# Attention inside a transformer block: each product with V preceded by one transpose of the next head's probabilities, and the small memory products moved to the steps without products with V

## The chip, the cores and the metric

The kernel runs on one core of a Trainium2 chip. The metric is the device time of one execution in microseconds (us). Times of the kernel before are the median of three runs; profiles are of one execution each. Engines are called as in the profile: PE is TensorE (its matmuls), PEld its loads of weights (the operand that stays in the array), DVE is VectorE, ACT ScalarE, POOL GpSimd, SP the engine that issues most transfers.

## What is computed

Layer norm, attention with a compressive memory, the output projection with its residual, and then a feed-forward block. The change is in the attention: 32 heads of 32 columns, four segments of 512 tokens, and within a segment a softmax over the segment's own keys, plus a reading of a memory that the earlier segments have filled.

```
def _A_ref(x, wq, wk, wv, wo, beta):
    B, S, D = x.shape
    H = 32; Dh = D // H; N = 4; L = S // N
    ...
    for s in range(N):
        qs, ks, vs = q[:, :, s], k[:, :, s], v[:, :, s]
        logits = jnp.einsum("bhqd,bhkd->bhqk", qs, ks) * scale + mask
        p = _softmax(logits, axis=-1)
        a_dot = jnp.einsum("bhqk,bhkd->bhqd", p, vs)
        pq = phi(qs)
        num = jnp.einsum("bhld,bhde->bhle", pq, M)
        den = jnp.einsum("bhld,bhd->bhl", pq, z)[..., None] + 1e-6
        a_mem = num / den
        o = g * a_mem + (1.0 - g) * a_dot
        outs.append(o)
        pk = phi(ks)
        M = M + jnp.einsum("bhld,bhle->bhde", pk, vs)
        z = z + jnp.einsum("bhld->bhd", pk)
    ...
    return o @ wo
```

Each segment reads M and z as the segments before it left them; the first reads nothing that counts, and the last need not write.

## The kernel before

All matrix work is done in float32 accuracy by halves: an operand is split into an upper part (names ending in h) and the rest (ending in l), and a product is the sum of the products of the parts.

The sequence is done in two halves of 1024 tokens, each of two segments. A **unit** is four heads (a group g of eight) of one segment, so there are 32 units. While the projections of one unit run on PE (`dense`: 24 steps t = 0 to 23, eight each for keys, queries and values, each step three 128x512 matmuls, L124 to L126, into `kps`, `qps`, `vps`), the heads of the unit before it are worked on in between: `interleave` takes one step of `dense`, then one step of `heads`, in turn. A head has six steps of its own (`slot`), and a head's work is spread over three such slots, so that three heads are under way at a time, one slot apart.

What is done in which step is set by the table `HEAD`: `q1=3.2` means that operation q with argument 1 is done in step 3 of a head, at place 2 among that step's operations; a time of 6 to 12 is one slot later, 12 to 18 two slots later. The operations:

- `q` (0 to 3): one block of 128 rows of the logits, a matmul into `pqk` (L659), DVE's scaling, mask and row extreme into `pr` (L660), ACT's exponential in place (L668). Block i has 128(i+1) keys.
- `t` (0 to 2): the transposes of the probabilities. Ten 128x128 blocks lie on or under the diagonal; they are turned on PE one by one (`ppt`, L709, against the identity `ident`) in groups of 4, 4 and 2, each group into one PSUM bank (two banks in turn, tag `pt`). After a group ACT copies it to `pth` (L711), and later `s` lets DVE compute the rest `ptl` (L716).
- `a` (0, 1): the products with V, eight matmuls for a head into `po` (L729), of 512, 512, 384, 384 columns in `a0` and 128, 128, 256, 256 in `a1`. The operand in the array is a 128x64 piece of `vs`.
- `o`: the sum of the halves of `po` and, with the fourth head, the gate and the addition of the memory's part. `w` is a small transpose `pw` (L688) with the fourth head, `r` the reciprocals.

**Small memory products** (L425): a unit that reads the memory has 12 matmuls `pm` (128x132), a unit that writes it 12 matmuls `pmm` (128x128). They are not done where they arise: `dense` puts them on a list `small` (the read at time 25 of the table `TIMES`, counted in steps from the unit's start, the update at time 40), and `one_small()` takes the next one from the list, if there is one. It is called ahead of each transpose (ten times a head) and ahead of each product with V but one (seven times a head). Two places empty the list in one go: `query_halves` (time 20) takes all that are left, and `memory_turn` (time 35) what the read still lacks. PE carries its instructions out in the order in which this recording writes them.

Of the kernel before, what the change touches and what calls it, by code (L numbers as in the profile page):

```python
# [17 lines left out]
P = 128  # L18
# [12 lines left out]
VT, KT, OT = True, True, True  # L31
WLC = 8
TIMES = dict(pk=10, kx=12, pkh=21, pkl=22, ks=11, qs=16, pq=16, pqh=20, pql=20, omt=20, vx=24, pm=25, vs=32, vl=33, pmm=40, om=35, omc=40, od=62, lk=13, lq=16, lv=20, ck=18, cq=22, cv=28)
HEAD = dict(r=6.1, q0=1.1, a0=14.1, s2=14.2, t0=8.3, q2=2.4, s0=8.5, a1=15.1, q1=3.2, t1=10.1, w=9.2, q3=4.3, t2=11.1, o=17.2, s1=11.3)
KD, QD = 0, 3
SCALE = DH ** -0.5
EPS = 1e-5
# [6 lines left out]
def raw(ap):  # L44
    return ap.bitcast(F32)


def build(tc, x, wq, wk, wv, wo, beta, w1, b1, w2, b2, out):
# [304 lines left out]
    def attention(half, first):  # L353
# [59 lines left out]
        def one_small():  # L413
            if small:
                small.pop(0)()
# [280 lines left out]
        def ptr(st, n):  # L696
            grp = ((0,), (1, 3), (2,))[n]
            if n == 0:
                st["pth"] = ab.tile([P, 1280], F32R, name="pth", bufs=2)
                st["ptl"] = ab.tile([P, 1280], F32R, name="ptl", bufs=2)  # L700
            pr, pth, ptl = st["pr"], st["pth"], st["ptl"]
            ppt = psum.tile([P, 512], F32, tag="pt", name="ppt", bufs=2)
            base = koff[grp[0]]
            w = 0
            for jk in grp:
                for i in range(jk, 4):
                    one_small()
                    o = koff[jk] - base + (i - jk) * P
                    nc.tensor.transpose(ppt[:, o:o + P], pr[:, offs[i] + jk * P:offs[i] + (jk + 1) * P], ident)  # L709
                    w += P  # L710
            acts["pth"] = n, nc.scalar.copy(pth[:, base:base + w], ppt[:, :w])  # L711
            st["sub", n] = (ptl[:, base:base + w], ppt[:, :w], raw(pth[:, base:base + w]))

        def sub(st, n):
            o, x0, x1 = st["sub", n]
            nc.vector.tensor_tensor(o, x0, x1, op=ALU.subtract)  # L716

        def av(st, n):
            u, j = st["u"], st["j"]
            if n == 0:  # L720
                st["po"] = psum.tile([P, 512], F32, tag="av", name="po", bufs=1)[0:64, :]
            po = st["po"]
            for jk in (0, 1) if n == 0 else (3, 2):
                w = 512 - P * jk
                v = u["vs"][:, 4 * j + jk, :]
                for part in ("pth", "ptl"):
                    if (jk, part) != (3, "ptl"):
                        one_small()
                    nc.tensor.matmul(po[:, P * jk:], v, st[part][:, koff[jk]:koff[jk] + w],  # L729
                                     start=(jk, part) == (0, "pth"), stop=(jk, part) == (2, "ptl"))  # L730
            if n == 1:
                if j == 0:
                    u["ot"] = ab.tile([P, 512], F32, name="ot", bufs=1)
                nc.scalar.copy(u["ot"][32 * j:32 * j + 32, :], po[32:64, :])
# [24 lines left out]

        stages = int(max(HEAD.values())) // 6  # L760
        pipe = [None] * stages
        fns = {"q": qk, "r": inverse, "w": weigh, "t": ptr, "s": sub, "a": av, "o": av_out}

        def slot(cur):
            states = [cur] + pipe
            for step in range(6):
                for _, op in sorted((t % 6, op) for op, t in HEAD.items() if int(t) % 6 == step):
                    st = states[int(HEAD[op]) // 6]
                    if st:
                        fns[op[0]](st, *[int(c) for c in op[1:]])  # L770
                yield
            pipe[:] = states[:-1]

        def heads(u):
            for j in range(4):
                yield from slot({"u": u, "j": j})

        def tail():
            for _ in range(stages):
                yield from slot(None)  # L780
# [682 lines left out]
    for half in range(2):  # L1463
        acts["zt"] = zt = tc.alloc_tile_pool(name=f"zt{half}", bufs=1, side="right")
        attention_pool(half)
        first = None if half else opening()
        rest = attention(half, first)
        hts = [lnp.tile([P, D], F32, tag="ln", name="ht0", bufs=4) for _ in range(4)]
        ab = acts["ab"]
# [132 lines left out]
```

## Time and profile before

| what | value |
| --- | --- |
| median of three runs | 2272.93 us (2271.5 to 2276.78) |
| span of the profiled execution | 2272.7 us |
| attention, first half of the sequence | about 46 to 490 us of the span |
| attention, second half | about 945 to 1390 us |
| transposes `ppt` | 1280 |
| products with V `po`, L729 | 1024 |
| small products `pm` and `pmm` | 288 and 288 |

How the views are read: the groups give, for a line, engine, operation and shape, the count, then the busy time in us and the mean duration of one in ns, then the idle time of the engine before them. A PE matmul's own duration there counts from its start to the end of its flow through the array, and the matmuls overlap: a 128x512 one is listed with some 390 ns although the next one ends 0.23 us after it. What a matmul adds to the time is therefore read from the chain of waits, which lists, in order of time, when each piece of work began to be the last thing that held the end up, and for how long: start in us, length in us, engine, tile and line, and a count where neighbours are merged.

### The profile page before, as it was taken

Reading aid. Unit: us, or ns where it says so; the run is one execution under the profiler, and the core shown is the slowest. Engines: PE = TensorE matmul, PEld = TensorE weight load, DVE = VectorE, ACT = ScalarE, POOL = GpSimd, SP = SyncE. Lnnn points to the kernel's source line nnn. Section 1 sums busy time; section 2 is a strip of 40 time slices with the busy share of each in tenths; the row PEclk is TensorE's granted clock in tenths of the full one; section 3 lists DMA queues with packets and bytes.
Section 4 is the critical chain, followed back from the end, with each engine's and each line's share of the span. In section 5 each row is a group of like instructions: output and inputs, shape, how many; then the busy total and the mean of one; then the engine's idle time right before and its main releaser. Section 6 shows DMA issues by size and latency. Waiting matters only on the chain.

```text
span 2272.7 us, 34849 instructions
## 1 busy us (share of the span) xinstructions
PE 2243.7 (99%) x11481; PEld 1861.9 (82%) x11481; DVE 1541.0 (68%) x3073; ACT 1232.8 (54%) x2553; POOL 856.8 (38%) x710
## 2 busy tenths in 40 slices
PE   8999999999999999999999999999999999999999
PEld 6888888877888888888888887888888888888887
DVE  6777777776656565777777787655666766567653
ACT  6777777774453445777777775453334223222221
POOL 4232233334244442233333334244445654055430
PEclk9999999999999999999999999999999999999999
DMA  6666666665475655666655565466568975476762
GB/s 215 182 190 181 181 179 176 177 177 196 139 212 165 189 167 173 195 177 179 178 173 169 178 195 189 142 210 181 162 177 310 331 253 197 155 257 226 244 234 89
DMA packets 400798, 437.41 MB, mean 192 GB/s; under 512 B 33102, under 2 KB 267114, under 8 KB 400618
## 3 DMA queue, kind: packets, MB, share of 16 engines
q1 hardware_dynamic: 337450, 398.48, 56.8%
q10 hardware_dynamic: 63168, 36.71, 5.4%
q8 instruction: 91, 1.49, 0.3%
q14 instruction: 89, 0.73, 0.1%
HBM read 287.41 MB, written 128.78 MB: 183 GB/s over the span
## 4 chain that ended last, share of the span: by engine, by line
PE 86%; DMA 4%; POOL 3%; ACT 2%; DVE 2%; issue 1%; SPq 1%; POOLq 0%; ACTq 0%; DVEq 0%
PE po L1436 22%; PE bps L1040 10%; PE cps L1040 7%; PE dps L1040 7%; PE po L729 6%; PE ppt L709 5%; PE pqk L659 3%; PE qps L124 3%; PE qps L125 2%; PE kps L124 2%; PE qps L126 2%; PE vps L124 2%; PE kps L126 2%; PE kps L125 2%; PE vps L125 2%; PE vps L126 2%
## 5 line engine op out<-in xcount | busy, mean ns | idle before, releaser
L668 ACT ACTIVATE pr<-pr,mx 128x128 f32<-128x128 f32 (+3 forms) x512 | 289.1, 565 | 107.3 <-DVE mx L660 104.0
L660 DVE CUSTOM_DVE_ANT_0 pr<-pqk,mask 128x128 f32<-128x128 f32 (+3 forms) x512 | 247.2, 484 | 87.0 <-PE pqk L659 82.2
L711 ACT CAST pth<-ppt 128x512 fp32r<-128x512 f32 (+1 forms) x384 | 194.9, 512 | 91.3 <-PE ppt L709 88.9
L716 DVE TENSOR_TENSOR ptl<-ppt,pth 128x512 fp32r<-128x512 f32 (+1 forms) x384 | 226.8, 595 | 14.5 <-ACT pth L711 11.9
L709 PE MATMUL ppt<-ident,pr 128*128 128x128 f32 x1280 | 217.4, 276 | 0.7 <-DVE ptl L716 0.4
L1446 DVE TENSOR_TENSOR c<-c,po 128x512 f32<-128x512 f32 x160 | 105.4, 683 | 149.0 <-PE po L1436 147.2
L709 PEld LDWEIGHTS ppt<-ident,pr 128*128 128x128 f32 x1280 | 163.9, 140 | 36.7 <-issue 2.2
L659 PE MATMUL pqk<-ks,qs 96*128 96x128 f32 (+3 forms) x512 | 183.0, 358 | 1.1 <-DVE mx L660 1.1
L799 POOL TENSOR_TENSOR wl<-wr,wh 128x1024 fp32r<-128x1024 f32 x42 | 101.1, 2406 | 179.1 <-ACT wh L797 132.0
L729 PE MATMUL po<-ptl,vs 128*64 128x512 f32 (+3 forms) x512 | 153.1, 308 | 1.9 <-DVE ptl L716 1.9
L729 PE MATMUL po<-pth,vs 128*64 128x512 f32 (+3 forms) x512 | 147.8, 309 | 2.9 <-DVE ot L740 1.6
L1436 PE MATMUL po<-w2h,zh 128*128 128x512 f32 x378 | 121.0, 390 | 0.2 <-DVE zh L1376 0.2
L1040 PE MATMUL bps<-zh,sb 128*128 128x512 f32 x336 | 111.1, 391 | 0.0
L1293 POOL TENSOR_TENSOR w2r<-w2r 128x512 f32<-128x512 f32 x54 | 85.4, 1590 | 68.3 <-DMA w2r<-in_B_w 45.4
L1040 PE MATMUL bps<-zh,sa 128*128 128x512 f32 x336 | 110.9, 391 | 0.0
L124 PE MATMUL kps<-yh,wh 128*128 128x512 f32 (+1 forms) x264 | 109.9, 416 | 0.0
L124 PE MATMUL qps<-yh,wh 128*128 128x512 f32 x256 | 107.8, 421 | 0.0
L124 PE MATMUL vps<-yh,wh 128*128 128x512 f32 x256 | 106.2, 415 | 0.0
L659 PEld LDWEIGHTS pqk<-ks,qs 96*128 96x128 f32 x512 | 98.2, 192 | 8.3 <-DVE mx L660 1.8
L1436 PE MATMUL po<-w2h,hl 128*128 128x512 f32 x322 | 103.3, 390 | 0.4 <-DVE hl L1376 0.4
L125 PE MATMUL kps<-yl,wh 128*128 128x512 f32 (+1 forms) x264 | 102.8, 389 | 0.1
L126 PE MATMUL kps<-yh,wl 128*128 128x512 f32 (+1 forms) x264 | 102.9, 390 | 0.0
(251 smaller groups left out, 6527.8 us busy)
## 6 DMA issues: line engine op xcount, KB each, us to landing
hr<-h_dram SPq DMA_DIRECT2D x112, 448.0 KB, 5.3
w2r<-in_B_w SPq DMA_DIRECT2D x122, 256.0 KB, 4.3
r<-in_B_w SPq DMA_DIRECT2D x56, 512.0 KB, 4.5
ks<-ks_dram SPq DMA_DIRECT2D x128, 192.0 KB, 3.1
h_dram<-ht ACTq DMA_DIRECT2D x84, 256.0 KB, 3.7
ks_dram<-kh SPq DMA_DIRECT2D x64, 256.0 KB, 2.6
wr<-in_A_wo SPq DMA_DIRECT2D x32, 512.0 KB, 4.5
wx<-in_B_w SPq DMA_DIRECT2D x56, 256.0 KB, 3.5
```

Of the source, the lines that this page charges most:

```text
L124: nc.tensor.matmul(ps, ah, bh, start=first, stop=False)
L125: nc.tensor.matmul(ps, ah, bl, start=False, stop=False)
L126: acts["mm"] = nc.tensor.matmul(ps, al, bh, start=False, stop=last)
L659: nc.tensor.matmul(pqk[:, :n], u["qs"][j][:, i * P:(i + 1) * P], u["ks"][j][:, 0:n], start=True, stop=True)
L660: nc.vector.tensor_tensor_reduce(out=st["pr"][:, offs[i]:offs[i] + n], in0=pqk[:, :n], in1=mask[:, 512 - n:512], op0=ALU.add, op1=ALU.min, ...
L668: nc.scalar.activation(pi, pi, AF.Exp, bias=mx[:, i:i + 1], scale=-1.0, accum_out=mx[:, 4 + i:5 + i])
L709: nc.tensor.transpose(ppt[:, o:o + P], pr[:, offs[i] + jk * P:offs[i] + (jk + 1) * P], ident)
L711: acts["pth"] = n, nc.scalar.copy(pth[:, base:base + w], ppt[:, :w])
L716: nc.vector.tensor_tensor(o, x0, x1, op=ALU.subtract)
L729: nc.tensor.matmul(po[:, P * jk:], v, st[part][:, koff[jk]:koff[jk] + w], start=(jk, part) == (0, "pth"), stop=(jk, part) == (2, "ptl"))
L1040: nc.tensor.matmul(ps, x_[:, c, :], y_[:, c, :], start=first and c == 0 and n == 0, stop=last and c == 3 and n == 2, skip_group_check=True)
L1436: nc.tensor.matmul(ps, x_[:, k], y_[k], start=opens and k == 0 and i == 0, stop=closes and k == self.KP - 1 and i == 2, skip_group_check=True)
```

## The change

The ten transposes and eight products of a head are put in another order, and the small products are called for at other places. One transpose of the head one slot younger now stands ahead of each product with V (`mixed`, as steps `m0` and `m1` of the table). One product goes without, the second one of 128 columns (`ptl` of key block 3, as with the small products before); in its stead a transpose follows on the last product of `m1`. The third group, of two, stays in its step, with a small product after each transpose. Two small products are called for at the beginning of each of the steps 0, 1 and 4, and none in the steps 2 and 3 as long as there are transposes. Times of the table follow: the second group of transposes is one step earlier (10.1 to 9.1, as part of `m1`), its `s1` too, the third block's `s2` is at 12.2 instead of 14.2.

```
-HEAD = dict(r=6.1, q0=1.1, a0=14.1, s2=14.2, t0=8.3, q2=2.4, s0=8.5, a1=15.1, q1=3.2, t1=10.1, w=9.2, q3=4.3, t2=11.1, o=17.2, s1=11.3)
+HEAD = dict(r=6.1, q0=1.1, m0=14.1, q2=2.4, s0=8.5, m1=15.1, q1=3.2, w=9.2, q3=4.1, s1=10.3, t2=11.1, o=17.2, s2=12.2)
...
             for jk in grp:
                 for i in range(jk, 4):
-                    one_small()
                     o = koff[jk] - base + (i - jk) * P
                     nc.tensor.transpose(ppt[:, o:o + P], pr[:, offs[i] + jk * P:offs[i] + (jk + 1) * P], ident)
                     w += P
+                    if w < P * sum(4 - k for k in grp):
+                        yield
             acts["pth"] = n, nc.scalar.copy(pth[:, base:base + w], ppt[:, :w])
             st["sub", n] = (ptl[:, base:base + w], ppt[:, :w], raw(pth[:, base:base + w]))
+            yield
+
+        def turns(st, n):
+            for _ in ptr(st, n):
+                one_small()
...
                 for part in ("pth", "ptl"):
                     if (jk, part) != (3, "ptl"):
-                        one_small()
+                        yield
                     nc.tensor.matmul(po[:, P * jk:], v, st[part][:, koff[jk]:koff[jk] + w],
...
-        fns = {"q": qk, "r": inverse, "w": weigh, "t": ptr, "s": sub, "a": av, "o": av_out}
+        fns = {"q": qk, "r": inverse, "w": weigh, "t": turns, "s": sub, "o": av_out}
+
+        def mixed(out, turn, n):
+
+            t = ptr(turn, n) if turn else iter(())
+
+            def short():
+                if next(t, t) is t:
+                    one_small()
+
+            if out:
+                for _ in av(out, n):
+                    short()
+            for _ in t:
+                pass

         def slot(cur):
             states = [cur] + pipe
             for step in range(6):
+                if step in (0, 1, 4):
+                    one_small()
+                    one_small()
                 for _, op in sorted((t % 6, op) for op, t in HEAD.items() if int(t) % 6 == step):
                     st = states[int(HEAD[op]) // 6]
-                    if st:
+                    if op[0] == "m":
+                        mixed(states[2], states[1], int(op[1]))
+                    elif st:
                         fns[op[0]](st, *[int(c) for c in op[1:]])
                 yield
```

On PE, in a slot without small products, step 2 (with the products of `a0`) and the start of step 3. Before:

```order
L126 MATMUL qps<-yh_204,wl 128x512
L729 MATMUL po<-pth,vs 64x512
L729 MATMUL po<-ptl,vs 64x512
L729 MATMUL po<-pth,vs 64x384
L729 MATMUL po<-ptl,vs 64x384
L709 MATMUL ppt<-ident,pr 128x128 x4
L659 MATMUL pqk<-ks,qs 128x384
```

Now:

```order
L126 MATMUL qps<-yh_204,wl 128x512
L708 MATMUL ppt<-ident,pr 128x128
L735 MATMUL po<-pth,vs 64x512
L708 MATMUL ppt<-ident,pr 128x128
L735 MATMUL po<-ptl,vs 64x512
L708 MATMUL ppt<-ident,pr 128x128
L735 MATMUL po<-pth,vs 64x384
L708 MATMUL ppt<-ident,pr 128x128
L735 MATMUL po<-ptl,vs 64x384
L659 MATMUL pqk<-ks,qs 128x384
```

The same eight instructions stand between the same neighbours; the run of four transposes is dealt out over the four products.

On PE, step 3 of such a slot, now (before, the four products stand there alone, in the same order, and the four transposes stand in a run in step 4):

```order
L126 MATMUL kps<-yh_204,wl 128x512
L708 MATMUL ppt<-ident,pr 128x128
L735 MATMUL po<-pth,vs 64x128
L735 MATMUL po<-ptl,vs 64x128
L708 MATMUL ppt<-ident,pr 128x128
L735 MATMUL po<-pth,vs 64x256
L708 MATMUL ppt<-ident,pr 128x128
L735 MATMUL po<-ptl,vs 64x256
L708 MATMUL ppt<-ident,pr 128x128
L688 MATMUL pw<-ident,rs 16x128
L659 MATMUL pqk<-ks,qs 128x256
```

Here a transpose follows directly on a 128-column product once.

On PE, the small products of a memory read (`mzh`, `mzl` are the memory's parts, `pqh`, `pql` the queries'). Before, the first of the twelve:

```order
L126 MATMUL kps<-yh_204,wl 128x512
L425 MATMUL pm<-mzh,pqh 128x132
L729 MATMUL po<-pth,vs 64x512
L425 MATMUL pm<-mzl,pqh 128x132
L729 MATMUL po<-ptl,vs 64x512
L425 MATMUL pm<-mzh,pql 128x132
L729 MATMUL po<-pth,vs 64x384
```

Now, six of the twelve, in steps 4, 5 and 0:

```order
L425 MATMUL pm<-mzh,pql 128x132
L425 MATMUL pm<-mzh,pqh 128x132
L659 MATMUL pqk<-ks,qs 128x512
L124 MATMUL kps<-yh_204,wh 128x512
L125 MATMUL kps<-yl_205,wh 128x512
L126 MATMUL kps<-yh_204,wl 128x512
L708 MATMUL ppt<-ident,pr 128x128
L425 MATMUL pm<-mzl,pqh 128x132
L708 MATMUL ppt<-ident,pr 128x128
L425 MATMUL pm<-mzh,pql 128x132
L124 MATMUL kps<-yh_204,wh 128x512
```

Before, a small product has a transpose or a product with V on each side; now most stand in pairs, between a matmul of the projections and one of the projections or of the logits.

## The prediction

> **What bounds the kernel now.** I read the page first, for the share of each engine, then who PE waits for, then the stretch of the attention.
>
> ```profile
> PE 2243.7 (99%) x11481; PEld 1861.9 (82%) x11481; DVE 1541.0 (68%) x3073; ACT 1232.8 (54%) x2553; POOL 856.8 (38%) x710
> ```
> ```profile
> PE po L729 <- DVE ptl L716: 1.9, 2, 1.1
> PE ppt L709 <- DVE ptl L716: 0.4, 2, 0.2
> ```
> ```profile
> 46.00:490.00 444.00, 443.40 (x2657) 372.00 (x2656) 338.87 (x964) 340.51 (x856) 139.06 (x145) 1.00 0.63 181
> ```
>
> PE is busy 99% of the span. In the whole run its products with V wait 1.9 us for the low halves and its transposes 0.4 us; in the first half's attention (46 to 490 us) PE is busy for 443.40 of 444.00 us at a granted clock of 1.00, while DVE has 338.87 and ACT 340.51 us of work. So nothing is to be won from waits, and the other engines have a quarter of their time spare. The change adds and removes no instruction: it is decided by what a matmul costs between its new neighbours.
>
> **What a matmul costs by its neighbours.** This is read from the chain of waits (start, length, what). Transposes first, in a run between 512-column matmuls, and a run with products with V behind it:
>
> ```profile
> 181.21 0.80 PE po L729 x4
> 182.01 0.44 PE ppt L709 x4
> 182.45 0.18 PE pqk L659
> ...
> 183.32 0.35 PE po L729 x4
> ```
> ```profile
> 500.74 0.43 PE ppt L709 x4
> 501.17 0.36 PE po L729 x4
> 501.53 0.12 PE pqk L659
> ```
>
> Four transposes take 0.44 us, 0.11 each, though a product of the same 128 columns takes half of that (the four of 0.35 are of 128, 128, 256 and 256 columns: 0.06, 0.06, 0.12, 0.12). Two things could make the 0.11: the transpose's own flow, or the load of the next 128x128 block, which cannot start before the block before it is in use. The second fence tells them apart: there the last of four transposes is followed by a product with V, whose 64-column operand loads within 0.06 us (a 128-column product behind another takes no more). Were it the load, the last transpose would cost 0.06 and the run 0.39. It costs 0.43, and the products behind it 0.36, as without transposes. **So a transpose flows for 0.11 us whatever follows.**
>
> Small products, among transposes and products with V:
>
> ```profile
> 68.55 0.23 PE kps L126
> 68.78 0.06 PE pm L425
> 68.84 0.23 PE po L729
> ...
> 69.84 0.06 PE pm L425
> 69.91 0.11 PE ppt L709
> 70.02 0.07 PE pm L425
> 70.09 0.13 PE ppt L709
> ...
> 70.61 0.20 PE pqk L659
> ...
> 71.55 0.12 PE po L729 x2
> 71.67 0.11 PE pm L425
> 71.79 0.12 PE po L729
> ```
>
> A small product between two products with V adds 0.06 us: its 128-column load is hidden by the product ahead, and the 64-column load behind it by its own flow. Behind a 128-column product, too short to cover that load, it adds 0.11. In a run of transposes, four small products and four transposes take from 69.84 to 70.61, 0.77 us, which is 0.33 more than the four transposes alone: 0.08 each. Now a small product next to another one, and a short matmul ahead of a projection:
>
> ```profile
> 180.59 0.62 PE pmm L425 x6
> ```
> ```profile
> 67.96 0.06 PE pqk L659
> 68.02 0.29 PE kps L124
> 68.31 0.23 PE kps L125
> ```
>
> Six small products in a run take 0.62: 0.06 for the last, behind which a 64-column load follows, and 0.11 for each of the others. They are bound by the next 128-column load. And a matmul of 128 columns ahead of a projection takes 0.06 and makes that one 0.29 instead of 0.23, so 0.12 in all.
>
> **The change part by part.** The counts:
>
> ```profile
> L709 PE MATMUL ppt<-ident,pr 128*128 128x128 f32 x1280 | 217.4, 276 | 0.7 <-DVE ptl L716 0.4 <-ACT pr L668 0.3
> L425 PE MATMUL pmm<-vs,pkh 128*128 128x128 f32 x192 | 39.9, 259 | 0.0
> L425 PE MATMUL pmm<-vs,pkl 128*128 128x128 f32 x96 | 27.8, 289 | 0.0
> L425 PE MATMUL pm<-mzh,pqh 128*128 128x132 f32 x96 | 24.9, 259 | 0.0
> ```
>
> Four transposes a head in `m0` (512 to 384 columns): 0.11 each, as in the run; their loads are hidden, but they were not what cost. Nothing won or lost. Four in `m1`: the same, but the one that follows directly on the second 128-column product has only 0.06 us of cover for its load. The nearest rows are the transposes behind small products: the first costs 0.11, the later ones 0.13. So 0 to 0.02 us, 128 times: 0 to 2.6, I take **+1.5 us**. The two of the third group are counted with the small products.
>
> Small products of a read, now, for the twelve: between the products with V 0.06 x 4, then 0.33 for the four in the transposes, then 0.06, 0.11, 0.06 among the last products and 0.06 ahead of a run of transposes: 0.86 us. Twenty-four units read (three segments of eight groups; 24 x 12 = 288, three kinds of 96): 20.6 us. Those of an update, now: four and two in transposes, at 0.08, then, in the 16 units whose list is emptied ahead of a read, the run of six: 0.48 + 0.62 = 1.10. In the other eight, four between products and two more in transposes: 0.48 + 0.24 + 0.16 = 0.88. Together 24.6 us. **Both before: 45.2 us.**
>
> After: both kinds come as five pairs and one pair that alternates with the two transposes of the third group (for an update in the 16 units, two of the pairs are one run of four, at the same price). A pair between two projections: 0.11 for the first (the second's load), 0.12 for the second (row of 68.02). Ahead of a block of logits, as the load is of 128 columns too, 0.11 and 0.11. I take 0.225. The alternating pair: each small product behind a transpose at 0.08, and the second has a projection behind it instead of a transpose, 0.12: 0.20. Twelve cost 5 x 0.225 + 0.20 = 1.325 us, and 48 sets **63.6 us. The difference is +18.4 us.**
>
> No operation is new to the trace; only the pair between projections is not in it as such. Its bounds: no less than 0.17 (one load hidden, 0.06 and 0.11), no more than 0.24 (0.12 twice), which for 240 pairs is -13 and +4 us. I stay at 0.225, as the run of six shows five loads in a row with none hidden.
>
> The Trainium skill, in "TensorE: Matmul & The Clock Gate", section "Back-to-back issue gap", gives an isolated warm matmul of 128 columns 128/2.4 + 2.5, about 56 ns; by it a transpose with a hidden load would take half of the 0.11 that the run shows. The same page, Part 4, says that a transpose does not get the full clock, and 128 columns at its half clock are an estimate of 107 ns, near the 0.11 of the rows; by this the sum above stands.
>
> What else moves: the second group's transposes and its `ptl` come a step earlier, the third group's `ptl` two steps; the copies on ACT and the subtractions on DVE keep at least one step (three 0.23 us projections and more) to the next user of their PSUM bank, so I cost them at nothing. Without that cover a wait would be of the size in the list of waits, 1.9 us in all. The last products of a read now come six steps later, in step 4 of the second head, just ahead of the place where the list would be emptied for it, so `om` is turned as before; its way through memory has until the fourth head's end, four heads later. The first transpose ahead of a product with V covers 0.11 us of waits for `po`; those are about 3 us in all at most, which I leave in the lower bound.
>
> The sum, against the profiled execution's span of 2272.7 us (0.2 us from the median of 2272.93): 2272.7 + 18.4 + 1.5 = 2292.6, **forecast 2292 us**, slower by 0.85%. Its own range, from the bounds (pairs -13, +4; transposes behind 128 columns -1.5, +1.1; waits -3, +3), not all at one end: 2281 to 2299.
>
> **The rivals.** *A transpose between products gets cheap.* If the 0.11 is the load of the next 128x128 block, a transpose behind a product with V, loaded while that one flows, and with a 64-column load behind it, costs 0.06: eight a head, 1024 times 0.05, 51 us less. With the small products' 18 the time is 2272.7 - 51 + 18 = 2240. For it: small products behind one another are bound just so. Against: 500.74, where the last of four costs 0.11 with a 64-column load behind it. The place is steps `m0` and `m1`; it decides from 0.09 us a transpose downwards, where 1024 x 0.02 outweighs the 18 us. The rule of the 56 ns cited above is this rival's.
>
> *Changing between kinds costs.* Transposes are plain f32, products fp32r; each change could cost what separates 0.13 from 0.11 in the rows at 70.09 and 69.91, 0.02 us. Some 900 changes more each way would bring 18 us on top: 2311. Against: the single step from products to transposes and back at 500.74 costs nothing.
>
> *No net change.* A transpose gets just 0.02 us cheaper (part of its 0.11 is hidden by the longer neighbours), and pays for the small products: 2272. Nothing in the rows speaks for it but the spread of 0.11 to 0.13.
>
> **How the numbers follow.** Forecast 0.80, first rival 0.09, second 0.06, third 0.05. The range for 8 of 10 holds the forecast's own and a little of what lies on both sides: 2277 to 2303. 0.2%, about 4.5 us, is what a measurement of this kernel can tell from no change: faster 0.10 (the first rival and a part of the third), same 0.05, slower 0.85.
>
> **What would show it.** In the changed kernel's chain of waits, within `m0`, `ppt` should show 0.11 and `po` 0.23 or 0.17, in alternation; 0.06 for `ppt` is the first rival, 0.13 or a longer `po` the second. Pairs of small products should show 0.06 and 0.11, with the matmul behind them 0.05 to 0.06 longer than its like. PE's waits should stay under some 30 us in all; new ones on `po`, `ppt` or the banks of the projections would make the forecast wrong on the slow side. The attention of each half should be about 10 us longer, and the feed-forward stretches as long as now.

## The result, and the profile after

The changed kernel takes 2299.51 us (median of four runs, 2295.20 to 2303.44), the kernel before beside it 2273.76 us: a ratio of 1.0105, with an interval of 1.0082 to 1.0127. It is slower by 25.7 us, inside the range forecast (2277 to 2303) and 7.5 us above the forecast of 2292. Measured a second time in another comparison the ratio is 1.0099 (1.0080 to 1.0118), 2296.22 against 2273.70 us, 22.5 us slower. The profiled execution is the slowest of the four, with a span of 2301.7 us (29.0 more than that of before), and the one profiled in the second comparison, at 2302.93 us, is the slowest of six (2292.17 to 2302.93), so the waits read below are those of slow executions.

The page's line of the engines, after:

```profile
PE 2266.6 (98%) x11481; PEld 1884.5 (82%) x11481; DVE 1533.3 (67%) x3073; ACT 1227.3 (53%) x2553; POOL 851.3 (37%) x710
```

As many instructions on every engine as before, and PE busy 22.9 us longer (it was 2243.7). The other 6.1 of the 29.0 us are time in which PE stood. From the first value projection (`vps`) of a half to its first output projection (`pwo`) PE takes 465.1 instead of 453.9 us in the first half and 469.9 instead of 454.6 in the second; the rest of the run is only some 2 us longer. Now the chain of waits, in a slot with the small products of a read (start, length, engine, tile and line):

```profile
67.16 0.17 PE pm L425 x2
67.33 0.11 PE pqk L659
67.44 0.28 PE kps L124
...
68.18 0.11 PE ppt L708
68.29 0.23 PE po L735
68.52 0.11 PE ppt L708
68.63 0.23 PE po L735
68.86 0.11 PE ppt L708
68.97 0.18 PE po L735
69.14 0.11 PE ppt L708
69.25 0.17 PE po L735
...
70.30 0.11 PE ppt L708
70.41 0.12 PE po L735 x2
70.52 0.14 PE ppt L708
...
72.05 0.17 PE pm L425 x2
72.22 0.29 PE pqk L659
```

Each of the prices is there. A transpose between products with V costs 0.11 us, as in a run, and the products keep their 0.23 and 0.17 to 0.18; the four pairs of 68.18 to 69.43 take 1.25 us, as the 0.44 of the run of four and the 0.80 of the four products took before. The transpose behind two 128-column products costs 0.14. A pair of small products takes 0.06 and 0.11, and makes what follows 0.05 to 0.06 longer (`pqk` of 128 columns 0.11 instead of 0.06, of 512 columns 0.29 instead of 0.23): 0.22 to 0.23.

What the order alone costs is read where nothing waits. The timeline of PE has, in the kernel before, the start of the same projection seven units apart (first column; the second is the matmul's own duration),

```profile
235.22 0.40 PE L124 MATMUL vps<-yh,wh 128*128 128x512 f32 x1
...
444.95 0.40 PE L124 MATMUL vps<-yh,wh 128*128 128x512 f32 x1
```

and after

```profile
241.29 0.40 PE L124 MATMUL vps<-yh,wh 128*128 128x512 f32 x1
...
455.29 0.39 PE L124 MATMUL vps<-yh,wh 128*128 128x512 f32 x1
```

209.73 us have become 214.00: 0.61 us a unit, which over the 31 units that have the heads of another beside them is 18.9 us. In the second half two units take 60.93 us where nothing waits, instead of 59.83, which is 0.55 a unit, so the order costs 18 to 19 us in all. The rest, some 10 us of the profiled execution and 4 to 7 us of the medians (22.5 and 25.7 less 18.9), is not order. PE's waits together went from 24.5 to 30.9 us. The longest of the output projection (`pwo`, for the parts of its operands) come to 7.4 us where they were 7.5 before. Those that grew most are, after,

```profile
PE ppt L708 <- DVE ptl L722: 4.0, 8, 1.1
...
PE pqk L659 <- DVE mx L660: 2.1, 1, 2.1
...
PE po L1461 <- DVE c L1471: 1.7, 1, 1.7
```

The first, the transposes' wait for a low half, was 0.4 us. The second was

```profile
PE pqk L659 <- DVE mx L660: 1.1, 2, 0.9
```

and the third, in the feed-forward part, is not in the list of before. A second part stands in no list of waits: the mean granted clock of TensorE went from 0.998 to 0.996 of full speed, by estimate 5 us (0.4% of 2301.7 less 0.2% of 2272.7 us). What that looks like is seen behind the wait of `pqk`, in the last section.

### The profile page after: what moved, and what is told of

Its sections match the earlier page's. It is cut to its first block, busy times and chain, and to the rows that moved or that the text cites. A ratio compares the mean times of both kernels' runs of the same rounds, so it can differ in the third digit from the quotient of the medians.

```text
span 2301.7 us, 34990 instructions
## 1 busy us (share of the span) xinstructions
PE 2266.6 (98%) x11481; PEld 1884.5 (82%) x11481; DVE 1533.3 (67%) x3073; ACT 1227.3 (53%) x2553; POOL 851.3 (37%) x710
## 4 chain that ended last, share of the span: by engine, by line
PE 81%; DMA 6%; DVE 3%; ACT 3%; POOL 3%; issue 2%; SPq 1%; ACTq 0%; POOLq 0%; DVEq 0%
PE po L1461 21%; PE bps L1065 9%; PE cps L1065 7%; PE dps L1065 6%; PE po L735 5%; PE ppt L708 5%; PE pqk L659 3%; PE vps L124 2%; PE vps L126 2%; PE vps L125 2%; PE qps L124 2%; PE kps L124 2%; PE qps L125 2%; PE qps L126 2%; PE kps L125 2%; PE kps L126 2%
## 5 line engine op out<-in xcount | busy, mean ns | idle before, releaser
L708 PE MATMUL ppt<-ident,pr 128*128 128x128 f32 x1280 | 314.9, 276 | 4.0 <-DVE ptl L722 4.0
L708 PEld LDWEIGHTS ppt<-ident,pr 128*128 128x128 f32 x1280 | 179.9, 141 | 30.4 <-issue 7.1
L735 PE MATMUL po<-pth,vs 128*64 128x512 f32 (+3 forms) x512 | 192.3, 388 | 2.5 <-DVE vs L539 1.8
L735 PE MATMUL po<-ptl,vs 128*64 128x512 f32 (+3 forms) x512 | 188.8, 370 | 0.0
L659 PE MATMUL pqk<-ks,qs 96*128 96x128 f32 (+3 forms) x512 | 177.7, 348 | 2.2 <-DVE mx L660 2.1
L735 PEld LDWEIGHTS po<-pth,vs 128*64 128x64 f32 x512 | 73.2, 143 | 36.6 <-DVE vs L539 3.2
```

The lines of the kernel that those rows point to most:

```text
L659: nc.tensor.matmul(pqk[:, :n], u["qs"][j][:, i * P:(i + 1) * P], u["ks"][j][:, 0:n], start=True, stop=True)
```

## The experiments

The theory to test had three parts: the small products cost because in pairs they wait for each other's load; the transposes dealt out cost little; and what other engines do stays hidden. All ratios are to the kernel before, run beside each.

**The pairs alone.** Transposes in runs as before, the small products where the change calls for them:

```
                 for i in range(jk, 4):
-                    one_small()
...
+                    if n == 2:
+                        one_small()
...
                     if (jk, part) != (3, "ptl"):
-                        one_small()
...
             for step in range(6):
+                if step in (0, 1, 4):
+                    one_small()
+                    one_small()
```

> The kernel before with its transposes in runs, and only the small products moved: pairs at the start of steps 0, 1 and 4, one behind each transpose of the third group. Theory (the pairs cost, since each small product waits for the next 128-column load; the order of the transposes costs almost nothing): most of the loss is here, 11 to 18 us over the kernel before, 2285 to 2292. Rival 1 (dealing the transposes out over the products is what costs): 2274 to 2279. Rival 2 (all of the loss, the waits included, comes from the small results being late): as the changed kernel, about 2299.

2293.86 us, 1.0080 (1.0062 to 1.0097). About three quarters of the change's loss (1.0099 and 1.0105) comes with the pairs alone, and the first rival, by which this would have been the time of before, falls. The second rival's 2299 lies above the interval too. The dealing out of the transposes, with the times of the table that were moved with it (`s1`, `s2`, `q3`), is left with 0.2%, some 5 us. The time is just above the theory's 2285 to 2292: here too something besides the order is lost. Where nothing waits, two units take 60.63 us in the first half and 60.56 in the second, against 59.76 and 59.83 before: 12 to 13 us of order in all, so some 6 of the 18.9 us (2293.86 less 2274.99) are not order. In the changed kernel two units take 60.97 and 60.93 us, 5 to 6 us more in all than here, which is as much as the time shows.

**Small products between a transpose and its product.** This keeps the change's order of the large work and takes the pairs away. Seven small products a head stand between a transpose and a product; two more, which the expectation does not count, still follow the two transposes of the third group:

```
-                if step in (0, 1, 4):
-                    one_small()
-                    one_small()
...
             def short():
-                if next(t, t) is t:
-                    one_small()
+                next(t, None)
+                one_small()
...
-pmm=40
+pmm=36
```

> The changed order of transposes and products with V, but each small product stands between a transpose and its product with V (seven a head), and the update is put on the list at time 36 instead of 40, so that few are left to be emptied in a run. Theory: a small product costs 0.06 there, as its load lies under the transpose and the next load under itself; with the transposes at 0.11 as ever this is 2268 to 2274. Rival 1 (the alternation costs): still 2287 or more. Rival 2 (lateness): the read ends about as late as in the changed kernel, so no less than 2285.

2294.43 us, 1.0082 (1.0070 to 1.0094), 20 us above the theory. In its chain the prices are what was expected for those between a transpose and a long product:

```profile
199.87 0.23 PE po L735
200.10 0.11 PE ppt L708
200.21 0.06 PE pm L425
200.27 0.23 PE po L735
```

Here a small product adds 0.06. But the list of waits has one that the kernel before has not:

```profile
PE pw L688 <- DVE om L551: 5.6, 22, 1.1
```

Two units take some 60.2 us in the first half and 60.5 or more in the second (59.76 and 59.83 before), so even the stretch between the ends of the attention has not become cheaper. The time does not decide between the rivals, as both named 2285 or more: the first has the 0.11 and the 0.23 of these rows against it, and lateness was not tested by itself. What `pw` waits for is seen in the next run.

**Transposes in runs, small products at the products with V alone**, `pmm=36`:

```
                 for i in range(jk, 4):
-                    one_small()
                     o = koff[jk] - base + (i - jk) * P
...
-pmm=40
+pmm=36
```

> The kernel before, transposes in runs, with the small products ahead of products with V alone (seven a head, none among the transposes), the update at time 36. Theory: 0.06 each but behind the 128-column product; no 0.08 among transposes and hardly a run at 0.11: 6 to 7 us below the kernel before, 2265 to 2269. Against small_between it shows the order of the transposes alone: 2 to 5 us less here. Rival 1: as theory here, but some 18 us less than small_between. A rival by which small products are hidden anyway in the kernel before: 2274.

2285.33 us, 1.0043 (1.0028 to 1.0059): slower than before, where 6 to 7 us less were expected. PE's waits show the same new one, and longer:

```profile
PE pw L688 <- DVE om L551: 8.3, 23, 1.6
PE pwo L125 <- POOL zl L101: 3.1, 2, 1.7
```

`pw`, the small transpose of the reciprocals, needs a PSUM bank that a read product of the same steps still holds until DVE has read it; PE stands for it 23 times, and 24 units read. Two units take 59.93 and 60.55 us in the two halves, so the 6 to 7 us that the sum of prices promised are not left even there. Against the kernel with the small products between, which is 9 us slower, the dealing out of the transposes differs, but also the table's times that were moved with it and the two small products a head in the third group.

**The same two with `pw` a step later** (`w=9.2` becomes `w=10.9`).

> As runs_small_at_products, with the small transpose of the reciprocals (w) a step later, at 10.9 instead of 9.2, when the bank of the first read product is free again. That kernel's PE waited 8.3 us for it in 23 units. Theory (the order there is 6 to 7 us cheaper than before, and what it lost were waits that it made itself): 8 to 9 us less than its 2285, about 2277. If the waits only move to the next matmul: 2283 to 2286.

> As small_between (one transpose ahead of each product with V, a small product between them), with the small transpose of the reciprocals at 10.9. Beside runs_small_pw_later only the order of transposes and products with V differs. Theory (a transpose costs 0.11 in either, but 0.02 to 0.03 more behind the second 128-column product): 2 to 5 us more than runs_small_pw_later. If dealing out the transposes hides their loads: some 50 us less. If the change of kinds costs 0.02 each: 15 us more or over.

2291.39 us, 1.0074 (1.0059 to 1.0090), and 2297.43 us, 1.0100 (1.0083 to 1.0116). The waits for `om` went from 8.3 to 4.4 us, and yet the first kernel became 6 us slower, with more waits at the end of the attention and in the projection behind it:

```profile
PE pwo L125 <- POOL zl L101: 4.5, 4, 1.8
PE pw L688 <- DVE om L551: 4.4, 5, 1.9
PE pqk L659 <- DVE mx L660: 4.0, 5, 1.4
PE pwo L124 <- ACT wh L100: 3.4, 3, 1.5
```

The expectation of 2277 is missed by 14 us. The pair still gives its difference: 6 us, where 2 to 5 were expected for the order of the transposes; the two intervals overlap, so the excess cannot be told, and here too the times and the third group differ as well.

**The update listed earlier, in the kernel before** (`pmm=40` becomes `pmm=36`, nothing else).

> The kernel before, with one number changed: the update's products on the list at time 36 instead of 40, so that hardly any are left for the run that is emptied ahead of a read (six at 0.11 in 16 units). Theory: 4 us less on PE, 2269 to 2272, if no wait is made. If the update's operands are not ready four steps earlier, PE waits for them, and it is 2274 or more.

2276.60 us, 1.0006 (0.9997 to 1.0015): no change that can be told. The order does save what was expected, as two units take 59.53 and 59.60 us instead of 59.76 and 59.83, some 3.5 us in all; it is not in the time. Where it is lost was not located.

**What makes the waits of the changed kernel?** Four edits were tried, each at one suspect. First, ACT's cast of the turned keys (`pkh=21, pkl=22` become 26 and 27):

> The changed kernel, with the upper half of the turned keys (ACT) five steps later, at 26 and 27 instead of 21 and 22, so that ACT no longer stands still until their transfer lands. Theory (of the loss, some 17 us are the order on PE, and the rest are waits, among them those of ACT for this transfer, 9.8 us in the first half against 2.5 before): 2291 to 2297, with PE no longer waiting for the low halves at 129 and 191 us of the span. If the waits come from elsewhere: 2299 as before.

2299.32 us, 1.0107 (1.0093 to 1.0122): no gain. But in its profile ACT still stands 9.0 us for that transfer in the first half, against 9.8, and the transposes still wait for low halves between 120 and 200 us, 1.4 us against 1.7. The edit left the wait in place that it was aimed at, so the suspicion was not put to the test. Then the read listed earlier (`pm=25` becomes `pm=22`):

> The changed kernel with the memory read put on the list at time 22 instead of 25, so that its twelve products stand in the same pairs, but the last of them a little over half a head earlier. On PE the order costs what it does in the changed kernel, some 17 us. If the waits beyond that (5 to 12 us in the profiled execution) come from the read's late end: 2290 to 2294. If they do not: 2297 to 2301.

2298.05 us, 1.0104 (1.0088 to 1.0121): no gain that the spread can tell. In its profile the transposes' wait for low halves is 2.3 us instead of 4.0 and that of `pqk` is not listed any more, but the read's products now wait for the parts of the memory, 1.6 us for `mzh` and 1.3 for `mzl`: some waits went and others came. Then the low half of the third group of transposes back at its old time (`s2=12.2` becomes `s2=14.2`), and beside it the changed kernel once more:

> The changed kernel with the low half of the third group back at 14.2 (it was moved to 12.2), so that DVE has its work in the order in which the kernel before has it at that place. On PE nothing changes, some 17 us over before. If the waits of the changed kernel's transposes for the low halves (4.0 us) come from that move: 2 to 4 us less than the changed kernel, 2295 to 2297. If not: 2298 to 2301.

> The changed kernel once more, beside the one above and with a second profile: the time again, 2296 to 2302, and the order on PE as in the first profile (a transpose 0.11 us, a pair of small products 0.22 to 0.23). If the waits at the ends of the attention are of chance, they stand at other places or have other lengths; if the order makes them, at the same.

2307.17 us, 1.0137 (1.0119 to 1.0155), against 2296.22 us, 1.0099 (1.0080 to 1.0118). The move of `s2` was not a loss but a help, of some 9 us. The second profile of the changed kernel speaks against chance: the transposes' wait for low halves is 3.3 us in 7 places (4.0 in 8 before), and the wait of the logits stands at the same place. Its chain near the end of the second attention,

```profile
1366.11 5.39 DMA orr<-o_dram
1371.50 0.02 issue
1371.52 0.43 DVE oh L869
1371.95 0.60 DVE pq L390
1372.55 0.47 DVE pr L660
...
1373.08 0.50 PE pqk L659
```

stands within 1 us of the place where the first profile has it:

```profile
1366.68 4.26 DMA orr<-o_dram
...
1370.97 0.43 DVE oh L869
1371.39 0.60 DVE pq L390
1371.99 0.47 DVE pr L660
```

A head's output is loaded for the projection that comes next, DVE stands for it in its order, the logits behind it wait, and PE with them. The last edit went at the issue of that load: SP stands before it for the store of a unit's output (`od=62` becomes `od=66`), in the changed kernel and, as a control, in the kernel before:

> The changed kernel with one number changed: the store of a unit's output (od) is issued at time 66 instead of 62. In the changed kernel SP, which issues its transfers in order, stands for POOL's last addition ahead of that store (24.1 us in the first half, 11.3 before), and what is queued behind it, the loads for the output projection among them, lands late; DVE and then PE wait for these (2.5 to 3.5 us at 1370 us). If that is where the waits beyond the order on PE come from: 3 to 6 us less than the changed kernel, 2291 to 2295, and no wait of PE over 1.5 us at the end of the second half's attention. If not: 2296 to 2301.

> The kernel before with the store at 66 instead of 62, as a control: there SP stands less for it, so no change beyond 2 us, 2272 to 2276, by either theory.

2298.36 us, 1.0103 (1.0090 to 1.0116), and 2276.14 us, 1.0004 (0.9994 to 1.0014): no gain in either. The wait that the edit was aimed at is still in its profile,

```profile
1362.45 4.64 DMA orr<-o_dram
...
1368.67 0.79 PE pqk L659
```

and PE waits 2.5 us ahead of this `pqk`, where no more than 1.5 was expected. So moving the store does not bring the load in earlier against the work around it; that the landing of the load makes this wait is what the chains show, and no run took it away.

## Why the prediction was right, and which terms were off

**The bound.** PE's order sets the steady part, as forecast: 0.61 us a unit in the first half and 0.55 in the second, 18 to 19 us in all, against the 19.9 of the sum (18.4 + 1.5). The signs named for it hold in part: the attention of the halves is 11 and 15 us longer, where about 10 was said, and the rest of the run 2 us. The sum comes so near partly by luck, as its two terms are off in opposite directions.

**Small products.** A pair at 0.225 and an alternating one at 0.20 were forecast; the chain has 0.22 to 0.23 for a pair. Comparing the steps with small products with the same steps without (from the start of a step's first projection matmul to that of the next step, median over the units), the twelve of a read cost 0.91 us before and 1.32 after, where 0.86 and 1.325 were forecast; those of an update 1.08 and 1.27 in the 16 units with the run, and 0.85 and 1.31 in the other eight. Together they are 45.8 us before and 62.3 after: 16.5 us more, so the term of 18.4 was some 2 us too large. That the pairs alone cost 18.9 us in time agrees with it by chance: 12 to 13 of these are order.

**Transposes.** That they cost 0.11 wherever they stand was right; it rested on a single place of the trace, and the chain after shows it in every slot. Their one dearer place, behind the two 128-column products, was put at 0 to 0.02 and shows 0.03 (0.14 against 0.11); over whole steps without small products it is 0.02 a head, 2.4 us in all instead of 1.5. Of the differences in time between kernels with the transposes in runs and dealt out, the 5 us between the pairs alone and the whole change are matched by order, as two units are 0.34 to 0.37 us longer (though the whole change also has the earlier `s2`, which a run of its own puts at some 9 us of help). This is more than the 2.4 because the pair of step 4 stands ahead of a run of transposes there, where it costs 0.15 to 0.21, and ahead of logits in the changed kernel, where it costs 0.22 to 0.23. The 9 and 6 us of the other two pairs of kernels were not taken apart.

**The first rival**, a transpose at 0.06, and **the second**, a cost for each change of kind in the steps with long products, are refuted by the chain after: a step 2 without small products takes 2.18 us before and 2.17 to 2.19 after, with the same eight instructions in turn instead of in two runs. The 0.14 is found only where the product ahead is short, at which load and change of kind cannot be told apart. **The third** is refuted by the time.

**What was hidden.** Here a step failed, though not by enough to leave the range. From a PE busy for 99%, with DVE and ACT idle for a quarter of their time, I had concluded that moves on other engines cost nothing, with 3 us either way. The copies on ACT and the subtractions on DVE, which were to keep their distance to the next user of the bank, were put at nothing; the transposes' wait for the subtraction's low halves went from 0.4 to 4.0 us, and to 3.3 in the second profile. In all the changed kernel lost 4 to 7 us beside the order in its medians and some 10 in its profile, where PE's waits, at 30.9 us, just pass the 30 that were named as a sign. And the two kernels whose order on PE was to be cheaper than that of before by the sum of prices, by 6 to 7 and by up to 5 us, were 10 and 19 us slower than it. A quarter of idle time is an average: with three PSUM banks shared by the projections and the small products, two for the transposes, and DVE and ACT each working in one order, when an instruction stands decides whether it is hidden. That waits of this kind are made by the order is shown, by the new wait for `om` and by the same waits in two profiles. Which of the change's moves makes those of the changed kernel stays open. With the cast and the store the wait aimed at stayed in place, so these two runs say little; the earlier read took some waits away and brought others; and the low half's move is a gain.

## What to carry to other kernels

Short matmuls with a wide stationary operand are cheap only where their load has cover: in this kernel next to each other they cost the load (0.11 us), behind a long matmul and ahead of one with a narrow operand they cost their flow (0.06). Before dealing out work to hide a load, find a place in the trace where the load is already short (here the transpose ahead of a 64-column operand, still at 0.11), and see whether the time goes away. And in a kernel whose order has been balanced against a few shared banks, a sum of PE's prices is a sum for PE; what the new order makes of the waits has to be measured, and can outweigh it.

## What the runs showed of the hardware

A wait of PE can be dearer than it looks. Behind the wait for the logits at 1372 us in the first profile of the changed kernel, its chain has

```profile
1372.52 0.79 PE pqk L659
1373.32 0.43 PE vps L124
1373.74 0.43 PE vps L125
1374.17 0.43 PE vps L126
1374.60 0.43 PE ppt L708 x2
1375.03 0.43 PE pwo L124
1375.45 0.43 PE pwo L125
1375.88 0.25 PE pwo L126
1376.13 0.23 PE pwo L124
```

For some 3.4 us each 512-column matmul takes 0.43 instead of 0.23, and then it is 0.23 again; the granted clock is 0.50 from 1372.4 to 1375.8 us and 1.00 just before and behind, and that of the whole execution fell with such stretches to 0.996. This one costs about half its length, 1.7 us, on top of the wait. The Trainium skill, "TensorE: Matmul & The Clock Gate", section "What's actually happening", describes such a gate, half clock for a window of about 3.4 us; the length agrees with these rows. That section lets it close after a whole idle window, and the idle time listed ahead of this one is 2.1 us.

The length of the wait does not decide it. In the second profile PE stands 3.1 us at the same place, and the clock stays at 1.00:

```profile
1373.08 0.50 PE pqk L659
1373.58 0.23 PE vps L124
1373.81 0.23 PE vps L125
```

In that execution the next stretch at half clock follows a wait of 1.7 us, at 1398 us. So the same wait cost 1.7 us of clock in one execution and nothing in the other, and what decides it was not found here.
